# Retention in plain fp32 on parts of the array, with loads further ahead

## The chip, the cores and the metric

The kernel runs on one core of one Trainium2 chip. The metric is the device time of one execution in microseconds, median over several runs. The engines are TensorE (PE, with its weight loads shown apart as PEld), VectorE (DVE), ScalarE (ACT), GpSimd (POOL) and SyncE (SP); DMA transfers are issued from the queues of SP, ACT and POOL.

## The reference

Three layers follow one another. Inputs q, k and v have shape (8, 8, 576, 64): batch, heads, positions, head size.

```python
scores = q @ k.transpose / 8
gamma  = 1 - 2.0 ** (-5 - head)
ret    = scores * (gamma ** (i - j) where i >= j, else 0)
x      = (ret @ v), heads side by side           # 4608 rows of 512
# mixture of experts: one expert of 8 per row, by cosine similarity
e      = argmax(x/|x| @ emb/|emb|.T / tau)
y      = softmax weight of e * (relu(x @ w1[e]) @ w2[e])   # 512 -> 1024 -> 512
# dense layer
h      = y @ w_in ; out = (h * cos(h)) @ w_out             # 512 -> 2048 -> 512
```

## The kernel before

**Retention in chunks.** Each batch of 576 positions is cut into four chunks of 128 and a last one of 64 (`NCH` = 5). A chunk needs four products for its eight heads: masked scores within the chunk (k against q), a state (k times scaled v, added to the state so far), the inter-chunk part (state against q) and the intra-chunk part (scaled v against masked scores). The powers of gamma are split: v is scaled by `gk_s` on POOL ahead of the products (line 394), the output by `gq_s` on VectorE behind them (line 478), so the mask itself is one triangle.

**Units and layout.** q and k arrive with two heads on the 128 partitions (`qk`), k and v also with positions on the partitions (`kv`). `load_chunk` (line 364) issues one load of each per chunk from the SP queue; the main loop (line 641) loads `AHEAD` = 3 chunks ahead into four buffers. The scales `gq_s` are loaded one chunk's worth at a time by `load_consts` between those loads.

**Scores.** fp32 data are split in `prep_chunk` (line 378), one chunk ahead, into a high and a low fp32r part: k on ScalarE and POOL (`kx`), q on ScalarE and VectorE (`qbd`). q is laid out block-diagonally with zeros, so a matmul on the full array handles two heads, and `mm3` (line 83) multiplies high by high, high by low and low by high: 12 matmuls with 256 columns a chunk. A last chunk takes plain fp32 instead (line 429).

**State and outputs.** The state is computed for two heads at once on the full array (line 440), and its two diagonal blocks are added to the previous state in `sbd`. The inter-chunk part uses the block-diagonal state as weights (line 459), the intra-chunk part column halves of the array (line 462). The two half chunks of a pair of batches share one tile `xtail`, so 40 chunks make 36 row tiles of 128.

**Routing.** `project` (line 483) turns a row tile into row order and multiplies it by the expert embeddings, one chunk later. After a group of tiles (9, 9, 9, 5, 4) `route` and `route_rest` compute expert, rank and weight. `emit` (line 561) then, two tiles per chunk, scatters the row numbers to `idb` (POOL queue), scales the rows on ScalarE and stores them to `xd` from the SP queue. The order on POOL and ScalarE is fixed to follow the prepared chunk (`issue_after`).

**Into the experts.** After the third group, `load_rows` gathers the first 320 rows of expert 0; their transposes (`rows_to_x`, line 259) come in the last chunk, and the expert layers (lines 84 to 86) follow. Six weight pieces of expert 0 are loaded and split during the retention (`PIECE_AT`, `load_piece`, line 178). The order within each engine's queue is laid down by a planner that simulates the program; the order of the source decides where it has no reason to differ.

Of the kernel before, what the change touches and what calls it, by code (L numbers as in the profile page):

```python
# [53 lines left out]
def retention_moe_ffn(  # L54
# [72 lines left out]
    def norm_recip(T, ssq, out):  # L127
        """out = 1 / (sqrt(ssq) + 1e-6)"""
        g, r, a = T("nr_g"), T("nr_r"), T("nr_a")
        nc.vector.tensor_scalar(g, ssq, 1e-36, None, op0=ALU.max)  # L130
        nc.scalar.activation(r, g, AF.Ln)
        nc.scalar.activation(r, r, AF.Exp, scale=-0.5)
        nc.vector.tensor_tensor(a, r, r, op=ALU.mult)
        nc.vector.tensor_tensor(a, a, g, op=ALU.mult)
        nc.vector.tensor_scalar(a, a, -0.5, 1.5, op0=ALU.mult, op1=ALU.add)
        nc.vector.tensor_tensor(r, r, a, op=ALU.mult)
        nc.vector.tensor_tensor(r, r, ssq, op=ALU.mult)
        nc.vector.tensor_scalar(r, r, 1e-6, None, op0=ALU.add)
        nc.vector.reciprocal(out, r)
# [37 lines left out]

    def load_piece(src, a, pool=None):
        i = wcount[0]
        st = stage.tile([P, 1024], F32, tag="st", name=f"st{i}")  # L180
        nc.sync.dma_start(st.rearrange("p (a b) -> p a b", a=a) if a > 1 else st, src)
# [141 lines left out]
    with ExitStack() as actx:  # L323
# [14 lines left out]
        def load_consts(i):  # L338
            if i == 0:
# [4 lines left out]
                nc.gpsimd.memset(zero, 0)  # L344
            elif i <= NCH:
                nc.sync.dma_start(gq_s[:, i - 1], gq[:, i - 1])
# [3 lines left out]
        qbd = []  # L350
        for i in range(2):
            t = acon.tile([P, 2, NP, 2, CH], F32R, name=f"qbd{i}")
            for a in range(2):
                for j in range(2):
                    (nc.gpsimd if i or a else nc.vector).memset(t[(1 - j) * D : (2 - j) * D, a, :, j, :].bitcast(F32), 0.0)
            qbd.append(t)

        sbd = []
        for i in range(3):
            t = acon.tile([P, NP, P], F32, name=f"sbd{i}")  # L360
            nc.gpsimd.memset(t, 0.0)
            sbd.append(t)

        def load_chunk(b, c):
            n = CH if c < 4 else 64
            cols = slice(c * NP * CH, c * NP * CH + NP * n)
            tk = qkv.tile([P, 2, NP * CH], F32, tag="qk", name=f"qk_{b}_{c}")
            for a in range(2) if b == c == 0 else (slice(0, 2),):
                src = qk[b, a, :, cols]
                nc.sync.dma_start(tk[:, a, : NP * n], src if b == c == 0 else src.rearrange("a p n -> p a n"))  # L370
            tk = tk[:, :, : NP * n].rearrange("p a (h n) -> p a h n", h=NP)
            tv = qkv.tile([P, 2, H, D], F32, tag="kv", name=f"kv_{b}_{c}")
            nc.sync.dma_start(tv[:n].rearrange("p a h d -> p (a h d)"), kv[b, c * CH : c * CH + n, :])
            return tk, tv

        nq = [0]

        def prep_chunk(b, c, r):
            n = CH if c < 4 else 64
            tk, tv = r  # L380
            split = None
            if c < 4:
                qb = qbd[nq[0] % len(qbd)]
                nq[0] += 1
                kx = tp.tile([P, 2, NP, CH], F32R, tag="kx", name=f"kx_{b}_{c}", bufs=2)
                nc.scalar.copy(kx[:, 0], tk[:, 1])
                eng = nc.vector if b == c == 0 else nc.gpsimd
                eng.tensor_tensor(kx[:, 1], tk[:, 1], kx[:, 0], op=ALU.subtract)
                for j in range(2):
                    h = slice(j * D, (j + 1) * D)  # L390
                    state["act"] = nc.scalar.copy(qb[h, 0, :, j, :], tk[h, 0])
                    nc.vector.tensor_tensor(qb[h, 1, :, j, :], tk[h, 0], qb[h, 0, :, j, :], op=ALU.subtract)
                split = qb, kx
            state["pool"] = nc.gpsimd.tensor_tensor(
                tv[:n, 1], tv[:n, 1], gk_s[:n, c * H : (c + 1) * H].unsqueeze(2).to_broadcast([n, H, D]), op=ALU.mult
            )
            return tk, tv, split

        state = {"i": 0}
        tails = {}  # L400

        def blk(t, j):
            return t[j * D : (j + 1) * D, :, j * D : (j + 1) * D]

        def tri_f(n):
            return mask_s[:n, :n].unsqueeze(1).to_broadcast([n, 4, n])

        def chunk_scores(b, c, r):
            n = CH if c < 4 else 64
            tk, tv, split = r  # L410
            pr = []
            for a in range(2):
                sc = bank(f"sc{a}_{b}_{c}")
                t = tp.tile([P, 4, CH], F32, tag=f"p{a}", name=f"p{a}_{b}_{c}")
                if c < 4:
                    qb, kx = split
                    for p in (2 * a, 2 * a + 1):
                        mm3(
                            sc[:, (p % 2) * 256 : (p % 2 + 1) * 256],
                            lambda s: kx[:, s, p, :],  # L420
                            lambda s: qb[:, s, p].rearrange("p a n -> p (a n)"),
                            True,
                            True,
                        )
                    pr += [t[:, k, :] for k in range(4)]
                else:
                    h = slice(a * D, (a + 1) * D)
                    for p in range(NP):
                        MM(sc[:n, p * n : (p + 1) * n], tk[h, 1, p, :], tk[h, 0, p, :], start=True, stop=True)
                    pr += [t[:n, k, :n] for k in range(4)]  # L430
                nc.vector.tensor_tensor(
                    t[:n, :, :n], sc[:n, : 4 * n].rearrange("p (a n) -> p a n", a=4), tri_f(n), op=ALU.mult
                )
            prev = sbd[state["i"] % 3]
            if c < 4:
                st_ps = bank(f"st_{b}_{c}")
                k2, v2 = (tv[:, a].rearrange("p h d -> p (h d)") for a in range(2))
                for p in range(NP):
                    cols = slice(p * P, (p + 1) * P)
                    MM(st_ps[:, cols], k2[:, cols], v2[:, cols], start=True, stop=True)  # L440
                state["i"] += 1
                nxt = sbd[state["i"] % 3]
                sv = st_ps.rearrange("p (a b) -> p a b", a=NP)
                for j in range(2):
                    if c == 0:
                        nc.scalar.copy(blk(nxt, j), blk(sv, j))
                    else:
                        nc.vector.tensor_tensor(
                            blk(nxt, j), blk(sv, j), blk(prev, j), op=ALU.add
                        )  # L450
            return pr, prev

        def chunk_out(b, c, r, pr, prev):
            n = CH if c < 4 else 64
            tk, tv, split = r
            ot = bank(f"ot_{b}_{c}")
            if c > 0:
                for p in range(NP):
                    MM(ot[:, p * n : (p + 1) * n], prev[:, p, :], tk[:, 0, p, :], start=(p == 0), stop=False)
            for p in range(NP):  # L460
                for j in range(2):
                    MM(
                        ot[j * D : (j + 1) * D, p * n : (p + 1) * n],
                        tv[:n, 1, 2 * p + j, :],
                        pr[2 * p + j if c < 4 else NP * j + p],
                        start=(c == 0 and p == 0),
                        stop=(p == NP - 1),
                    )
            if c < 4:
                xt = xtp.tile([P, NP, P], F32, tag="xt", name=f"xt_{b}_{c}")  # L470
                o = 0
            else:
                g = b // 2
                if b % 2 == 0:
                    tails[g] = xtp.tile([P, NP, P], F32, tag="xtail", name=f"xtail_{g}", bufs=2)
                xt = tails[g]
                o = (b % 2) * 64
            nc.vector.tensor_tensor(
                xt[:, :, o : o + n], ot[:, : NP * n].rearrange("p (a b) -> p a b", a=NP), gq_s[:, c, :, :n], op=ALU.mult
            )  # L480
            return xt

        def project(t, xt, lp, ssq, i):
            xr = rows.tile([P, DM], F32, tag="xr", name=f"xr_{t}")
            for a in range(2):
                ps = bank(f"xn{a}_{t}")
                w = P + E
                for j in range(2):
                    p = 2 * a + j
# [493 lines left out]
```

## Time and profile before

| | us |
|---|---|
| median of 3 runs | 1576.01 (1574.17 to 1588.26) |
| profiled execution, span from its first to its last instruction | 1564.1 |
| TensorE busy in the span | 1492.1 (95%) |
| VectorE, ScalarE, POOL busy | 777.9, 629.0, 670.6 |

The page gives the span as the profiled execution's own time and no other. Retention ends at about 251 us of the span, the experts run to about 800 us and the dense layer to the end. Times in rows count from the span's start. "Idle before" names what the engine waited for. In a timeline, consecutive instructions of a kind are merged into one row; starts are measured, ends of matmuls are modelled.

### The profile page before, as it was taken

The numbers are of one execution on the slowest core, as the hardware profiler recorded it, in microseconds if no ns is written. First come the engines' busy times: TensorE is split into PE (matmuls) and PEld (weight loads), VectorE is DVE, ScalarE is ACT, GpSimd is POOL, SyncE is SP. The second block draws the span as 40 slices with busy tenths as digits, with TensorE's granted clock in tenths as the row PEclk, the third lists the DMA queues.
The fourth block names the chain that finished last, engine by engine and source line by source line (L and its number), as shares of the span: only waits on it lengthen the run. The fifth ranks groups of instructions, "written<-read, shape, count | busy, mean of one in ns | idle before, by whom it ended". The sixth has DMA issues, their size and how long they took to land.

```text
span 1564.1 us, 22887 instructions
## 1 busy us (share of the span) xinstructions
PE 1492.1 (95%) x8760; PEld 1326.3 (85%) x8760; DVE 777.9 (50%) x1357; ACT 629.0 (40%) x1120; POOL 670.6 (43%) x494
## 2 busy tenths in 40 slices
PE   8979897899999999999999999999999999999996
PEld 7968787799999899999988888888888888888885
DVE  7968685342745536556263434444444434444432
ACT  4556564242343333432363433434333334334332
POOL 5564755475565665653553223232323223232322
PEclk9998898999999999999999999999999999999998
DMA  9596974564555554544510100000000100000000
GB/s 306 180 207 208 225 185 83 148 189 151 174 169 165 168 181 162 169 153 140 192 55 7 41 7 27 27 28 27 27 28 21 34 1 27 27 28 0 28 1 27
DMA packets 118690, 157.50 MB, mean 101 GB/s; under 512 B 18984, under 2 KB 78760, under 8 KB 118576
## 3 DMA queue, kind: packets, MB, share of 16 engines
q1 hardware_dynamic: 109760, 134.58, 29.0%
q0 software_dynamic: 7360, 19.95, 3.9%
q8 instruction: 71, 1.16, 0.3%
q10 hardware_dynamic: 1456, 1.45, 0.3%
q14 instruction: 43, 0.35, 0.1%
HBM read 118.03 MB, written 38.06 MB: 100 GB/s over the span
## 4 chain that ended last, share of the span: by engine, by line
PE 51%; issue 1%; DVE 1%; ACT 0%; POOL 0%; DMA 0%; POOLq 0%; ACTq 0%; DVEq 0%
PE f L84 8%; PE f L86 8%; PE f L85 8%; PE o L84 8%; PE o L85 8%; PE o L86 8%; PE y L85 1%; PE y L86 1%; PE y L84 1%; PE h L85 0%; PE h L86 0%; PE h L84 0%; POOL g L855 0%; DMA wf<-ta 0%; DVE kk L847 0%
## 5 line engine op out<-in xcount | busy, mean ns | idle before, releaser
L855 POOL TENSOR_TENSOR g<-kk,g 128x512 fp32r<-128x512 f32 x143 | 184.5, 1291 | 509.2 <-ACT g L854 509.0
L187 POOL TENSOR_TENSOR w<-st,w 128x1024 fp32r<-128x1024 f32 x80 | 193.0, 2423 | 123.1 <-ACT w L186 119.1
L85 PE MATMUL o<-w,g 128*128 128x512 f32 x576 | 224.1, 389 | 0.0
L85 PE MATMUL f<-xf,w 128*128 128x512 f32 x576 | 224.1, 389 | 0.0
L86 PE MATMUL f<-xf,w 128*128 128x512 f32 x576 | 224.1, 389 | 0.0
L84 PE MATMUL o<-w,g 128*128 128x512 f32 x576 | 223.7, 389 | 0.2 <-DVE kk L852 0.2
L84 PE MATMUL f<-xf,w 128*128 128x512 f32 x576 | 222.5, 389 | 0.0
L850 ACT ACTIVATE sn<-kk 128x512 f32<-128x512 f32 x144 | 91.0, 632 | 320.9 <-DVE kk L848 320.5
L86 PE MATMUL o<-w,g 128*128 128x512 f32 x576 | 219.2, 389 | 0.0
L847 DVE TENSOR_SCALAR kk<-f 128x512 f32<-128x512 f32 x144 | 99.4, 691 | 230.0 <-PE f L86 221.4
L852 DVE SCALAR_TENSOR_TENSOR kk<-sn,f 128x512 f32<-128x512 f32 x144 | 98.8, 687 | 183.9 <-ACT sn L851 183.7
L85 PE MATMUL y<-hs,w 128*128 128x320 f32 x512 | 162.3, 317 | 11.6 <-DVE hs L289 11.6
L84 PE MATMUL y<-hs,w 128*128 128x320 f32 x512 | 162.7, 318 | 3.5 <-ACT hs L288 3.5
L86 PE MATMUL y<-hs,w 128*128 128x320 f32 x512 | 160.5, 314 | 0.0
L84 PE MATMUL h<-x,w 128*128 128x320 f32 x512 | 158.1, 309 | 2.4 <-PEq L725 2.4
L86 PE MATMUL h<-x,w 128*128 128x320 f32 x512 | 157.6, 308 | 0.0
L85 PE MATMUL h<-x,w 128*128 128x320 f32 x512 | 157.6, 308 | 0.0
L854 ACT CAST g<-kk 128x512 fp32r<-128x512 f32 x144 | 89.3, 621 | 113.6 <-DVE kk L852 112.8
L84 PEld LDWEIGHTS o<-w,g 128*128 128x128 f32 x576 | 108.1, 188 | 23.1 <-DVE kk L852 0.6
L86 PEld LDWEIGHTS f<-xf,w 128*128 128x128 f32 x576 | 108.2, 188 | 22.5
L85 PEld LDWEIGHTS o<-w,g 128*128 128x128 f32 x576 | 108.2, 188 | 22.4
L84 PEld LDWEIGHTS f<-xf,w 128*128 128x128 f32 x576 | 108.1, 188 | 22.4
(152 smaller groups left out, 2759.4 us busy)
## 6 DMA issues: line engine op xcount, KB each, us to landing
st<-in_moe_w_dram SPq DMA_DIRECT2D x64, 512.0 KB, 3.7
kv<-in_kv_dram SPq DMA_DIRECT2D x32, 512.0 KB, 9.1
qk<-in_qk_dram SPq DMA_DIRECT2D x31, 512.0 KB, 4.4
xs<-x2t SPq DMA_DIRECT2D x36, 256.0 KB, 2.9
x2t<-y SPq DMA_DIRECT2D x56, 160.0 KB, 3.1
xd<-xr SPq DMA_DIRECT2D x32, 256.0 KB, 9.8
sd<-in_moe_w_in_dram SPq DMA_DIRECT2D x16, 512.0 KB
wf<-ta SPq DMA_DIRECT2D x32, 256.0 KB, 2.7
```

The costliest lines, as they stand in the source:

```text
L84: keep(MM(ps, lhs(0), rhs(0), start=first, stop=False))
L85: keep(MM(ps, lhs(0), rhs(1), start=False, stop=False))
L86: keep(MM(ps, lhs(1), rhs(0), start=False, stop=last))
L187: nc.gpsimd.tensor_tensor(wt[:, 1], st, wt[:, 0], op=ALU.subtract)
L847: nc.vector.tensor_scalar(kk, ps, MAGIC, MAGIC, op0=ALU.add, op1=ALU.subtract)
L850: nc.scalar.activation(sn, kk, AF.Sin, scale=math.pi)
L852: evac = nc.vector.scalar_tensor_tensor(kk, sn, 0.5, ps, op0=ALU.subtract, op1=ALU.mult)
L854: lasti[:] = evac, nc.scalar.copy(gt[:, 0], kk)
L855: (nc.vector if (t, m) == seqf[-1] else nc.gpsimd).tensor_tensor(gt[:, 1], kk, gt[:, 0], op=ALU.subtract)
```

## The change

Scores, state and inter-chunk part become plain fp32 matmuls on parts of the array: scores on row halves (64 rows by 128 columns, one head each, halves taking turns), state on column halves (128 by 64), the inter-chunk part on quarters (64 by 64). All splits of q and k go, with the block-diagonal tiles `qbd` and `sbd`. Row and column halves exchange two heads, so `gq`, the row order in `project` and the embedding are permuted to match, and the output scale is applied in two instructions. The half chunks of two batches become one unit of 128 positions with a mask that keeps the batches apart; there are 36 units in place of 40 chunks. Loads run six units ahead with seven buffers, q and k of a unit lie together (4 KB per partition), the scales follow at distance two, `rows` has 14 buffers. The `xd` stores move from SP's queue to ScalarE's. Weight pieces are fetched at their place and split two units later. A projected tile follows one unit after its output.

```diff
+    def load_piece(src, a, pool=None):
+        return split_piece(fetch_piece(src, a, wcount[0]), pool)
...
-        rows = actx.enter_context(tc.tile_pool(name="rows", bufs=12))
+        rows = actx.enter_context(tc.tile_pool(name="rows", bufs=14))
-        qkv = qctx.enter_context(tc.tile_pool(name="qkv", bufs=4))
+        qkv = qctx.enter_context(tc.tile_pool(name="qkv", bufs=7))
...
+        def load_chunk(u):
+            tk = qkv.tile([P, 2, NP, CH], F32, tag="qk", name=f"qk_{u}")
+            for a in (slice(0, 1), slice(1, 2)) if u == 0 else (slice(0, 2),):
+                nc.sync.dma_start(tk[:, a], qk[u, :, a])
+            tv = qkv.tile([P, 2, H, D], F32, tag="kv", name=f"kv_{u}")
+            nc.sync.dma_start(tv.rearrange("p a h d -> p (a h d)"), kv[u])
...
-                nc.scalar.copy(kx[:, 0], tk[:, 1])
-                eng.tensor_tensor(kx[:, 1], tk[:, 1], kx[:, 0], op=ALU.subtract)
-                    state["act"] = nc.scalar.copy(qb[h, 0, :, j, :], tk[h, 0])
-                    nc.vector.tensor_tensor(qb[h, 1, :, j, :], tk[h, 0], qb[h, 0, :, j, :], op=ALU.subtract)
...
+        heads = [(p, a) for p in range(NP) for a in range(2)]
+        quads = [(m, a, j) for m in range(2) for a in range(2) for j in range(2)]
+        def lanes(a):
+            return slice(a * D, (a + 1) * D)
+        def chunk_scores(u, c, r):
+            sc = [bank(f"sc{a}_{u}") for a in range(2)]
+            for p, a in heads:
+                MM(sc[a][:, p * P : (p + 1) * P], tk[lanes(a), 1, p, :], tk[lanes(a), 0, p, :], start=True, stop=True)
...
+        def chunk_state(u, c, r, prev):
+            for p, a in heads:
+                MM(st_ps[lanes(a), p * D : (p + 1) * D], tv[:, 0, 2 * p + a, :], tv[:, 1, 2 * p + a, :], start=True, stop=True)
...
+                nc.vector.tensor_tensor(nxt, sv, prev, op=ALU.add)
...
+        def chunk_inter(u, c, r, prevs):
+            ot = [bank(f"ot{a}_{u}") for a in range(2)]
+            n = P // max(1, len(prevs))
+            for i, prev in enumerate(prevs):
+                for m, a, j in quads:
+                    MM(ot[a][lanes(j), m * P + i * n : m * P + (i + 1) * n],
+                       prev[lanes(a), p, :], tk[lanes(a), 0, p, i * n : (i + 1) * n], ...)
...
+        def chunk_out(u, c, r, pr, ot):
+            for m, a, j in [(m, a, j) for a in range(2) for m in range(2) for j in range(2)]:
+                MM(ot[a][lanes(j), m * P : (m + 1) * P], tv[:, 1, 2 * p + a, :], pr[a][:, p, :], ...)
+            for a in range(2):
+                nc.vector.tensor_tensor(xt[:, am, :], ot[a]..., gq_s[:, c, am, :], op=ALU.mult)
...
-                with tc.issue_after(state["pool"].ins), tc.issue_after(state["act"].ins):
+                with tc.issue_after(state["pool"].ins):
...
-                    nc.sync.dma_start(xd[row : row + P, :], xr)
+                    nc.scalar.dma_start(xd[row : row + P, :], xr)
...
-        AHEAD = 3
+        AHEAD = 6
         for i in range(AHEAD):
-            raw[seq[i]] = load_chunk(*seq[i])
-            load_consts(i)
+            raw[i] = load_chunk(i)
+            if i < 2:
+                load_consts(i)
...
+                load_consts(i + 2)
+                raw[i + AHEAD] = load_chunk(i + AHEAD)
             ...
+            pr = chunk_scores(i, c, r)
             tick(2)
...
+            ot = chunk_inter(i, c, r, [] if c == 0 else [prev] if c < NCH - 1 else [state[(b - 1, c - 1)], prev])
+            while pend:
                 rest = project_next(pend.pop(0))
...
+            if c < NCH - 1:
+                state[(b, c)] = chunk_state(i, c, r, prev)
+            xt = chunk_out(i, c, r, pr, ot)
...
+            if fetched and fetched[0][0] <= i - 2:
+                key, st = fetched.pop(0)[1:]
+                with tc.issue_after(state["pool"].ins):
+                    (w1p if key < 4 else w2p)[(0, key % 4)] = split_piece(st)
```

## Rows read from the trace of the kernel before

**Rows 1.** Windows, retention: TensorE, loads, VectorE, ScalarE, POOL busy; clock; DMA share, GB/s.

```profile
0.00:251.00 251.00, 214.09 (x1991) 194.39 (x1992) 187.95 (x425) 135.44 (x295) 135.38 (x123) 0.92 0.76 208
```

**Rows 2.** Windows, same columns: three stretches of the retention.

```profile
10.00:40.00 30.00, 27.90 (x261) 24.75 (x260) 24.20 (x48) 15.49 (x34) 14.23 (x12) 0.94 0.98 329
84.00:120.00 36.00, 23.07 (x200) 20.81 (x200) 23.43 (x34) 20.09 (x40) 24.05 (x21) 0.86 0.90 187
...
128.47:154.06 25.59, 25.21 (x259) 23.17 (x260) 23.89 (x67) 15.43 (x36) 9.95 (x9) 1.00 0.59 196
```

**Rows 3.** Timeline of TensorE, one chunk: start, length, line, shapes, count.

```profile
50.87 0.39 PE L84 MATMUL sc<-qbd,kx 128*128 128x256 f32 x1
...
51.68 1.05 PE L440 MATMUL st<-kv 128*128 128x128 f32 x8
52.57 1.09 PE L490 MATMUL xn<-rx,xt 128*128 128x136 f32 x8
53.50 1.05 PE L459 MATMUL ot<-qk,sbd 128*128 128x128 f32 x8
54.49 1.09 PE L462 MATMUL ot<-p,kv 128*64 128x128 f32 x16
55.51 0.56 PE L429 MATMUL sc<-qk 64*64 64x64 f32 x7
```

**Rows 4.** Timeline of TensorE, a half chunk, same columns.

```profile
33.72 1.00 PE L459 MATMUL ot<-qk,sbd 128*128 128x64 f32 x8
34.65 0.68 PE L462 MATMUL ot<-p,kv 64*64 64x64 f32 x16
35.26 0.51 PE L84 MATMUL sc<-qbd,kx 128*128 128x256 f32 x2
```

**Rows 5.** Timeline of all engines, 105 to 120; in brackets, idle before and releaser.

```profile
106.30 0.58 PE L86 MATMUL sc<-qbd,kx 128*128 128x256 f32 x1 [5.61 <-POOL kx L388]
...
109.42 7.31 DVE L392 TENSOR_TENSOR qbd<-qk,qbd 64x512 fp32r<-64x512 f32 x1 [9.82 <-ACT qbd L391]
...
118.91 1.34 PE L462 MATMUL ot<-p,kv 128*64 128x128 f32 x10 [6.33 <-DVE p L431]
```

**Rows 6.** Waits of the SP queue, 0 to 251: total us, times, longest.

```profile
SPq L370 <- PE ot L459: 49.5, 20, 4.8
SPq L575 <- ACT xr L570: 28.3, 16, 4.5
```

**Rows 7.** Lines by shape, 0 to 290: busy us, mean ns, idle before.

```profile
L392 DVE TENSOR_TENSOR qbd<-qk,qbd 64x512 fp32r<-64x512 f32 x64 | 67.8, 1060 | 30.0 <-ACT qbd L391 28.6
L431 DVE TENSOR_TENSOR p<-sc,misc_i 128x512 f32<-128x512 f32 x64 | 42.6, 683 | 10.3 <-PE sc L86 10.0
...
L388 POOL TENSOR_TENSOR kx<-qk,kx 128x512 fp32r<-128x512 f32 x31 | 39.7, 1282 | 50.3 <-ACT kx L386 50.1
...
L187 POOL TENSOR_TENSOR w<-st,w 128x1024 fp32r<-128x1024 f32 x12 | 29.2, 2443 | 9.3 <-ACT w L186 9.2
...
L448 DVE TENSOR_TENSOR sbd<-st,sbd 64x256 f32<-64x256 f32 x48 | 19.9, 415 | 2.0 <-PE st L440 1.4
...
L478 DVE TENSOR_TENSOR xtail<-ot,gq_s 128x256 f32<-128x256 f32 x8 | 3.4, 419 | 0.9 <-PE ot L462 0.9
```

**Rows 8.** Timeline of all engines, start: first load of scales, fourth scaled output.

```profile
3.90 0.33 SPq L346 DMA_DIRECT2D gq_s<-c_gq_dram  x1
...
32.20 0.69 DVE L478 TENSOR_TENSOR xt<-ot,gq_s 128x512 f32<-128x512 f32 x1 [0.62 <-PE ot L462]
```

**Rows 9.** Timeline of all engines, 237 to 260.

```profile
237.44 1.01 POOL L564 DMA_INDIRECT idb<-misc_i,di  x1 [0.16 <-issue]
...
243.10 0.39 SPq L244 DMA_DIRECT2D ix<-idb  x1
...
249.55 1.09 PE L266 MATMUL xt<-ident,nat 128*128 128x128 f32 x4 [6.83 <-DMA nat<-xd,ix]
...
259.59 0.40 PE L84 MATMUL h<-x,w 128*128 128x320 f32 x1
```

More of the change, by code (lines that the diff above doesn't have):

```diff
@@ L364, in load_chunk @@
[L364 to L373, printed above, removed]
+        mask_t = acon.tile([P, P], F32, name="mask_t")
@@ L394, in prep_chunk @@
             state["pool"] = nc.gpsimd.tensor_tensor(
-                tv[:n, 1], tv[:n, 1], gk_s[:n, c * H : (c + 1) * H].unsqueeze(2).to_broadcast([n, H, D]), op=ALU.mult
+                tv[:, 1], tv[:, 1], gk_s[:, c * H : (c + 1) * H].unsqueeze(2).to_broadcast([P, H, D]), op=ALU.mult
             )
[L397 to L406, printed above, removed]
@@ L411, in chunk_scores @@
             pr = []
             for a in range(2):
[L413 to L430, printed above, removed]
+                t = tp.tile([P, NP, CH], F32, tag=f"p{a}", name=f"p{a}_{u}")
@@ new lines, in chunk_scores @@
+                nc.vector.tensor_tensor(t, sc[a].rearrange("p (a n) -> p a n", a=NP), tri, op=ALU.mult)
+                pr.append(t)
+            return pr
+        def chunk_state(u, c, r, prev):
+            tk, tv = r
+            st_ps = bank(f"st_{u}")
+            for p, a in heads:
+                MM(
+                    st_ps[lanes(a), p * D : (p + 1) * D],
+                    tv[:, 0, 2 * p + a, :],
+                    tv[:, 1, 2 * p + a, :],
+                    start=True,
+                    stop=True,
+                )
+            nxt = tp.tile([P, NP, D], F32, tag="s", name=f"s_{u}", bufs=4)
+            sv = st_ps[:, : NP * D].rearrange("p (a b) -> p a b", a=NP)
+            if c == 0:
+                nc.scalar.copy(nxt, sv)
+            else:
+                nc.vector.tensor_tensor(nxt, sv, prev, op=ALU.add)
+            return nxt
@@ new lines, in chunk_inter @@
+        def chunk_inter(u, c, r, prevs):
+            tk, tv = r
+            ot = [bank(f"ot{a}_{u}") for a in range(2)]
+            n = P // max(1, len(prevs))
+            for i, prev in enumerate(prevs):
+                for m, a, j in quads:
+                    p = 2 * m + j
+                    MM(
+                        ot[a][lanes(j), m * P + i * n : m * P + (i + 1) * n],
+                        prev[lanes(a), p, :],
+                        tk[lanes(a), 0, p, i * n : (i + 1) * n],
+                        start=(m == 0 and i == 0),
+                        stop=False,
+                        skip_group_check=True,
+                    )
+            return ot
@@ new lines, in chunk_out @@
+        def chunk_out(u, c, r, pr, ot):
+            tk, tv = r
+            for m, a, j in [(m, a, j) for a in range(2) for m in range(2) for j in range(2)]:
+                p = 2 * m + j
+                MM(
+                    ot[a][lanes(j), m * P : (m + 1) * P],
+                    tv[:, 1, 2 * p + a, :],
+                    pr[a][:, p, :],
+                    start=(c == 0 and m == 0),
+                    stop=(m == 1),
+                    skip_group_check=True,
+                )
+            xt = xtp.tile([P, NP, P], F32, tag="xt", name=f"xt_{u}")
+            for a in range(2):
+                am = slice(2 * a, 2 * a + 2)
@@ L431, in chunk_scores @@
                 nc.vector.tensor_tensor(
-                    t[:n, :, :n], sc[:n, : 4 * n].rearrange("p (a n) -> p a n", a=4), tri_f(n), op=ALU.mult
+                    xt[:, am, :], ot[a][:, : 2 * P].rearrange("p (m q) -> p m q", m=2), gq_s[:, c, am, :], op=ALU.mult
                 )
[L434 to L480, printed above, removed]
@@ L487, in project @@
                 w = P + E
-                for j in range(2):
-                    p = 2 * a + j
-                    MM(ps[:, j * w : (j + 1) * w], xt[:, p, :], rx[:, p, :], start=True, stop=True)
+                for m in range(2):
+                    MM(ps[:, m * w : (m + 1) * w], xt[:, 2 * a + m, :], rx[:, 2 * a + m, :], start=True, stop=True)
                 pv = ps[:, : 2 * w].rearrange("p (a b) -> p a b", a=2)
@@ L600, in prepare_experts @@
                 nc.vector.tensor_copy(rx[:, c, :P], ident)
-        seq = [(b, c) for b in range(B) for c in range(NCH)]
+        seq = [(b, c) for b in range(B) for c in range(NCH) if c < NCH - 1 or b % 2]
         raw = {}
@@ L921, in _layout, with units @@
 def _layout(q, k, v):
-    t = [a.reshape(B, NP, P // D, S, D).transpose(0, 2, 4, 1, 3).reshape(B, P, NP, S) for a in (q, k)]
-    t = np.stack(t, axis=2)
-    t = t.transpose(0, 2, 1, 3, 4)
-    qk = np.concatenate([t[..., c * CH : (c + 1) * CH].reshape(B, 2, P, -1) for c in range(NCH)], axis=3)
-    kv = np.stack([a.transpose(0, 2, 1, 3) for a in (k, v)], axis=2).reshape(B, S, 2 * DM)
-    return dict(qk=qk, kv=kv)
+    def units(a, axis):
+        cut = [slice(c * CH, (c + 1) * CH) for c in range(NCH)]
+        at = lambda b, c: a[b][(slice(None),) * axis + (cut[c],)]
+        for b in range(B):
+            yield from (at(b, c) for c in range(NCH - 1))
+            if b % 2:
+                yield np.concatenate([at(b - 1, NCH - 1), at(b, NCH - 1)], axis=axis)
+    t = [a.reshape(B, NP, P // D, S, D).transpose(0, 2, 4, 1, 3).reshape(B, P, NP, S) for a in (q, k)]
+    qk = np.stack([np.stack(list(units(a, 2))) for a in t], axis=2)
+    kv = np.stack([np.stack(list(units(a.transpose(0, 2, 1, 3).reshape(B, S, DM), 0))) for a in (k, v)], axis=2)
+    return dict(qk=qk, kv=kv.reshape(NTILE, P, 2 * DM))
 def _consts():
```

84 lines of the change are left out of this document (35 added, 49 removed).

## The prediction

> **What bounds the kernel now.** I read the windows first. The retention stage, 0 to 251 us, keeps TensorE busy for 214.09 of 251 us at a mean granted clock of 0.92, with the DMA engines at a share of 0.76 [rows 1]. All that the change touches lies ahead of the first uninterrupted expert matmul at 259.59 [rows 9]; the 1304.5 us behind it I take over unchanged.
>
> Inside the stage there are two regimes. A batch without a disturbance, 128.47 to 154.06, has TensorE busy for 25.21 of 25.59 us at clock 1.00 [rows 2]: TensorE sets the pace, 25.6 us for four chunks and a half one. The timeline shows how a full chunk fills it, by differences of starts: scores in fp32r 0.81 us for six matmuls (1.62 for twelve), state 0.89, projection 0.93, inter-chunk part 0.99, intra-chunk part 1.02, together 5.4 us [rows 3]. The second regime is 84 to 120: TensorE busy 23.07 of 36 us, clock 0.86, DMA share 0.90 but only 187 GB/s, where 10 to 40 has 329 GB/s at share 0.98 [rows 2]. There the scores waited 5.61 us for POOL's split of k, and the next output 6.33 us for masked scores; these stood on VectorE behind one split of q that took 7.31 us [rows 5], where the mean is 1.06 [rows 7]. Eight batches at 25.6 are 205 us, so some 45 of the first 251 us are start-up, such stalls and the slow clock behind them.
>
> The SP queue shows why data come late: its q and k loads waited 49.5 us in all for old buffers to be read out, and the xd stores, in the same queue with the loads behind them, 28.3 us for ScalarE's scaling [rows 6].
>
> **The change, part by part.**
>
> *The splits of q and k go.* VectorE loses two instructions a chunk, 67.8 us in all; POOL loses 39.7 us [rows 7]; ScalarE its casts. VectorE keeps per unit two masks at 0.683, a state sum in one instruction (0.42) and the output scale in two halves (0.42 each, as the 256-column row) [rows 7]: 2.6 us and the routing's small ones, below any TensorE pace here. What is late next is TensorE itself, or the raw load.
>
> *TensorE.* In the trace an fp32 matmul is two instructions; eight of them on the full array take 0.89 us, 0.111 each [rows 3]. Column halves run side by side: sixteen take 1.02 us [rows 3], which is 16 x 0.056 and 0.13 more at the change of array shape. Quarters with 64 columns, two at once: sixteen in 0.61 us [rows 4], 0.038 each, or 16 x 0.028 and 0.17. I charge 0.15 for a change of shape. Per new unit:
> - State, sixteen on column halves with 64 columns: 0.61, as that row.
> - Output, column halves as before: 1.02. Projection as before: 0.93.
> - Inter-chunk, sixteen on quarters with 128 columns: between 0.028 (four at once) and 0.056 (two at once) each; I take the middle, 0.042, so 0.67 + 0.15 = 0.82.
> - Scores, sixteen on row halves with 128 weight columns: no row has row halves taking turns. Side by side they would cost 0.056 each, one by one 0.111. For the upper end speaks that the full-array inter-chunk part with 64 moving columns takes 0.93 us for eight [rows 4], hardly less than 0.99 with 128 [rows 3]: something other than the moving columns binds there. For the lower end speaks that quarters overlap. I take 0.076, twice the 0.038 of the 64-column quarter, the nearest row: 1.22 + 0.15 = 1.37.
>
> Sum 4.75 us, against 5.4 for a full chunk, and nine units replace ten chunks of two batches. A batch's first unit has no inter-chunk part (0.8 less, seven of the 30 units counted below), a joined unit no state, but 32 short inter matmuls (0.4 less, three): 6.8 us off in all. A unit changes the array's shape once or twice more than a chunk did, and the 0.15 is charged each time. The Trainium skill, TensorEngine Tiling (Array Packing), section Key Properties, says that a change of tiling mode drains the engine, which speaks against this change; it gives no price, and with a drain as long as the 0.15 us read from the rows the sum stays as it is.
>
> *Six units ahead, seven buffers, xd stores on ScalarE's queue.* The load of unit i+6 needs the buffer of unit i-1, long read out, and no store stands ahead of it. A store now stands on ScalarE behind its own scaling and delays what follows there; at 0.33 us an issue, as the 256 KB load shown [rows 8], two a unit in a burst are 0.7 us, covered by a ScalarE that is busy 15.43 of 25.59 us even with the casts [rows 2]. If that cover fails, the copies of the projection come 0.7 us later in some 14 burst units: 10 us at most. POOL's scatters no longer wait for ScalarE, only for the POOL scaling of the next unit's v, whose load is now early. Splitting a weight piece two units after its fetch moves POOL and ScalarE work off a landing; cost nothing, POOL being busy for 9.95 of 25.59 us [rows 2]; uncovered, 2.4 us for each of six pieces [rows 7].
>
> *Start-up, late next.* The output scales gq of chunks 1 to 3 used to be issued between the first loads; now the first of them stands behind six units, 6 x 1.05 MB, and 0.4 MB of constants, at 329 GB/s [rows 2] some 21 us after the first microsecond, and each next one behind one more unit (1.31 MB, 4 us). So the scaled outputs of units 1, 2 and 3 can't come before 22, 26 and 30 us, though no split stands ahead of the first scores any more. Before, the fourth came at 32.20 [rows 8]. I take 30.
>
> *DMA in the three bursts.* By the last load 51 MB have moved (37.7 q, k and v, 7.1 xd, 4.7 weight pieces, 1.5 constants). Nine units with a burst of stores are 12.6 MB: 38 us at 329 GB/s, under TensorE's 42. If 7.6 MB of them move at 187 GB/s it is 41 + 15 us, 14 late a cycle, 42 in three, of which the lead of six units (28 us) hides all but 14. I take 4, and keep 0 and 14.
>
> *End.* The chain keeps its length: last scatter of the third group at 237.44, its indices read from 243.10, first transposes at 249.55, dense expert matmuls at 259.59: 22 us [rows 9]. As before, one unit lies between scatter and transposes, so TensorE still waits there.
>
> **Sum.** 30 (fourth output) + 30 units x 4.75 - 6.8 + 1.4 (scores of the 35th unit) = 167; + 22 = 189; + 4 (bursts); + 3 for small waits (TensorE's 25.59 - 25.21 us a batch [rows 2], eight times) = 196 us for the first dense expert matmul, 64 us earlier than 259.59. The profiled span is 1564.1 us; the median of the runs is 11.9 more, which I take for what lies around the span. 1564.1 - 64 + 11.9 = **1512 us**.
>
> **Rivals.**
> - *Row halves don't overlap.* Scores at 0.111 and inter at 0.056 each: 0.8 us a unit more, 24 us: 1536. For it, the 64-column row above. The Trainium skill, TensorE: Matmul & The Clock Gate, section LDWEIGHTS, has a rule that would cause it: a weight load's time goes by its columns, not its rows, and the scores still load 128 columns; at its figure, an estimate of 107 ns a load, the time is about the same. The trace agrees on the full array alone. Chance 0.20.
> - *DMA late by its upper end.* The bursts cost 14 and the start-up 5 more: 1527. For it, the 187 GB/s; against it, the lead. Chance 0.16.
> - *Slower.* With a queue of their own the xd stores mix with the loads at all times, and the 187 GB/s of a burst becomes the stage's rate: 51 MB take 273 us, and with 18 us of the end chain behind the last load the experts start at 291, 31 us later than now: 1607. It decides from 211 GB/s down (51 MB in 241.6 us). Against it, the stage averages 208 GB/s with the DMA engines free for a quarter of the time [rows 1]. Chance 0.08.
> - *It doesn't do what it says.* Loads wait elsewhere (behind constants, for buffers), and the time saved on TensorE turns into waiting for data; only a part of the stalls goes, up to 11 of the 45 us: 1565 to 1576. Chance 0.08.
>
> **How the numbers follow.** The forecast has 0.48. Within 1% (1560 to 1592, about what a measurement can't tell from no change) lies the last case, slower the third: faster 0.84, same 0.08, slower 0.08. The low end takes 0.056 and 0.028 for the two open prices (16 us less), no late burst (4) and an earlier start (4): 1488. The high end takes serial row halves and late bursts together: 1546, and 4 more for ScalarE in the bursts: 1550.
>
> **What would show it.** Scores: sixteen row-half matmuls in 1.0 to 1.4 us if right, 1.8 or more if they don't overlap. Pace: outputs of neighbouring units 4.2 to 5 us apart in undisturbed stretches. TensorE waits over 5 us for data only in the first 30 us and once at the end. First dense expert matmul near 196, the same 1304 us behind it. I am wrong if windows between 60 and 160 us show TensorE well under 0.9 busy with a DMA share near 1, if the granted clock there lies for long at its lower level of 1.2 GHz, or if the expert stage grows.

## The result, and the profile after

| | before | after |
|---|---|---|
| median on the same chip, us | 1579.98 (1574.17 to 1588.26) | 1535.07 (1532.43 to 1535.38) |
| span of the profiled execution, us | 1564.1 | 1533.5 |
| first expert matmul of the profiled execution, us | 258.05 | 220.00 |

The ratio is 0.9714, 95% interval 0.9676 to 0.9753: faster by some 45 us, where 64 were forecast. 1535 lies inside the range, 23 above the predicted 1512. The experiments show that one thing costs more than the whole miss: the way the row numbers (ids) are scattered into their table. I had seen it in the trace of before and put it down to another cause. The 258.05 and 220.00 are the first expert matmuls of all, with the projection of the last tile still behind them. The prediction counts from 259.59, behind that projection and 1.5 us later, so its 196 answers to 194.5 here.

**Where the forecast holds.** The timeline of TensorE, one unit of after in a quiet stretch (start, length, line, shapes, count); it answers to [rows 3, 4]:

```profile
41.02 1.16 PE L386 MATMUL sc<-qk 64*128 64x128 f32 x16
42.12 0.67 PE L421 MATMUL ot<-qk,s 64*64 64x128 f32 x16
42.71 1.19 PE L458 MATMUL xn<-rx,xt 128*128 128x136 f32 x8
43.84 0.69 PE L399 MATMUL st<-kv 128*64 128x64 f32 x16
44.35 1.05 PE L435 MATMUL ot<-p,kv 128*64 128x128 f32 x16
```

By differences of starts: scores 1.10, inter-chunk part 0.59, projection 1.13, state 0.51, and 0.98 up to the next scores at 45.33: 4.31 us a unit. The fourth scaled output, which answers to the last of [rows 8], comes at 29.83 (VectorE's timeline; the first stands in the same view):

```profile
12.40 0.74 DVE L446 TENSOR_TENSOR xt<-ot,gq_s 128x256 f32<-128x256 f32 x2
...
29.83 0.86 DVE L446 TENSOR_TENSOR xt<-ot,gq_s 128x256 f32<-128x256 f32 x2
40.70 0.86 DVE L446 TENSOR_TENSOR xt<-ot,gq_s 128x256 f32<-128x256 f32 x2
```

**Where it does not.** Windows of after (the columns of [rows 1]): the retention stage, a quiet stretch, and the stretch with the first two groups of scatters.

```profile
0.00:251.00 251.00, 208.10 (x2707) 177.15 (x2708) 129.81 (x418) 96.41 (x232) 97.14 (x93) 0.89 0.74 223
...
145.00:175.00 30.00, 29.70 (x492) 25.44 (x490) 22.33 (x68) 10.60 (x30) 14.24 (x10) 0.98 0.86 311
...
66.00:145.00 79.00, 60.01 (x780) 49.13 (x776) 35.61 (x109) 30.73 (x74) 34.83 (x31) 0.85 0.92 219
```

VectorE and POOL have lost 58 and 38 us against [rows 1], about as forecast, though this window of after has some 30 us of the expert stage in it. But from 66 to 145 TensorE is busy for 60 of 79 us with the DMA engines at a share of 0.92 and only 219 GB/s. From the fourth output to the 34th (29.83 to 206.72) 30 units take 5.9 us each. In that stretch POOL issues nine scatters in a row, and TensorE does the scores of one unit in pieces (timelines of POOL and of TensorE; in brackets the idle time before and its end):

```profile
67.95 1.14 POOL L532 DMA_INDIRECT idb<-misc_i,di  x1 [0.32 <-DVE lp L463]
...
78.23 0.96 POOL L532 DMA_INDIRECT idb<-misc_i,di  x1 [0.31 <-issue]
```

```profile
72.58 0.64 PE L386 MATMUL sc<-qk 64*128 64x128 f32 x2
73.68 0.47 PE L386 MATMUL sc<-qk 64*128 64x128 f32 x3 [0.46 <-issue]
74.38 0.27 PE L386 MATMUL sc<-qk 64*128 64x128 f32 x1 [0.23 <-issue]
...
80.22 0.80 PE L386 MATMUL sc<-qk 64*128 64x128 f32 x3 [1.04 <-issue]
```

Sixteen matmuls that take 1.10 us elsewhere are spread from 72.58 to 81.0. "issue" says that nothing which the profile shows was waited for; the waits of TensorE, 0 to 224 us (total, times, longest), have 20.5 us of it, of which the three largest are

```profile
PE xn L458 <- issue: 6.5, 5, 2.2
PE sc L386 <- issue: 6.4, 12, 1.0
PE st L399 <- issue: 6.1, 6, 2.0
```

The end, answering to [rows 9] (all engines; the last scatter of the third group, the reading of its indices, the transposes, the first expert matmul):

```profile
188.99 0.96 POOL L532 DMA_INDIRECT idb<-misc_i,di  x1 [0.30 <-issue]
196.38 0.38 SPq L250 DMA_DIRECT2D ix<-idb  x1
...
211.25 1.48 PE L272 MATMUL xt<-ident,nat 128*128 128x128 f32 x12
...
220.00 0.64 PE L84 MATMUL h<-x,w 128*128 128x320 f32 x1
```

### The profile page after: what moved, and what is told of

It is laid out like the page before. It is cut to its first block, busy times and chain, and to the rows that moved or that the text cites. A ratio compares the mean times of both kernels' runs of the same rounds, so it can differ in the third digit from the quotient of the medians.

```text
span 1533.5 us, 23567 instructions
## 1 busy us (share of the span) xinstructions
PE 1456.4 (95%) x9272; PEld 1281.2 (84%) x9272; DVE 696.9 (45%) x1294; ACT 569.6 (37%) x1016; POOL 616.5 (40%) x450
## 3 DMA queue, kind: packets, MB, share of 16 engines
q8 instruction: 75, 1.23, 0.3%
## 4 chain that ended last, share of the span: by engine, by line
PE 53%; DVE 1%; issue 1%; DMA 1%; POOL 1%; ACT 1%; POOLq 0%; ACTq 0%; DVEq 0%
PE f L85 8%; PE f L84 8%; PE f L86 8%; PE o L84 8%; PE o L85 8%; PE o L86 8%; PE y L85 1%; PE y L86 1%; PE y L84 1%; DMA wf<-ta 1%; PE h L85 1%; PE h L86 1%; PE h L84 1%; POOL w L193 0%; POOL g L837 0%
## 5 line engine op out<-in xcount | busy, mean ns | idle before, releaser
L193 POOL TENSOR_TENSOR w<-st,w 128x1024 fp32r<-128x1024 f32 x74 | 177.9, 2415 | 120.3 <-ACT w L192 120.1
L84 PE MATMUL h<-x,w 128*128 128x320 f32 x512 | 160.1, 313 | 4.3 <-DVEq L707 4.3
L85 PE MATMUL h<-x,w 128*128 128x320 f32 x512 | 159.4, 311 | 0.0
L86 PE MATMUL h<-x,w 128*128 128x320 f32 x512 | 159.4, 311 | 0.0
```

Of the source, the lines that this page charges most:

```text
L84: keep(MM(ps, lhs(0), rhs(0), start=first, stop=False))
L85: keep(MM(ps, lhs(0), rhs(1), start=False, stop=False))
L86: keep(MM(ps, lhs(1), rhs(0), start=False, stop=last))
L193: nc.gpsimd.tensor_tensor(wt[:, 1], st, wt[:, 0], op=ALU.subtract)
```

## The experiments

Twelve kernels ran, in three sets, each set beside the kernel before on one chip; ratios are to that, and the changed kernel's own is 0.9714 (0.9676 to 0.9753). In the cuts of code, "..." stands for lines left out. One window, 66 to 145 us, compares them: in the changed kernel 780 matmuls, 219 GB/s.

My first theory (A) was that nine scatters in a row starve the other engines, since the change had removed the wait that spread them. Four kernels undo one part each.

**e1_paced**: scatters and row scalings again wait for ScalarE's last copy.

```diff
-                nc.scalar.copy(xv[:, a], ...)
+                state["act"] = nc.scalar.copy(xv[:, a], ...)
...
+                    tc.add_manual_dep(ins.ins, state["act"].ins.name, ..., reason="pace")
+                    with tc.issue_after(state["act"].ins):
-                    nc.scalar.mul(xr, xr, gt[:, i : i + 1])
+                        nc.scalar.mul(xr, xr, gt[:, i : i + 1])
```

> The changed kernel, with the pacing of the emits put back: each scatter on GpSimd and each scaling of a row on ScalarE is issued only behind the copy of the last projected tile on ScalarE, as in the kernel before; stores, lead and matmuls stay as in the changed kernel. Theory A (the nine scatters run back to back, from 67.95 to 79.2, 126.1 to 137.2 and 178.9 to 190 us, and beside them every engine is slow to get its instructions, at a loss of 10 to 13 us in a burst): the scatters come in small groups again, the three stretches shrink, and the first dense expert matmul comes at 185 to 200 us in place of 223.7; about 1505 us, ratio to before 0.955. Rival B (the loads and the stores on two queues share the DMA engines; scatters are innocent): the stretches stay, 1530 to 1540 us, ratio 0.97. Rival C (pacing keeps ScalarE or GpSimd waiting for the projection and holds up the next value scaling): slower than the changed kernel, 1540 to 1560 us.

Measured: 1542.86 us, ratio 0.9739 (0.9706 to 0.9771). The scatters of the first group did spread (two at 67 to 69 us, six from 80 to 88, one at 106), and the time did not fall. Windows, first 66 to 145, then a stretch with the last scatter of the first group:

```profile
66.00:145.00 79.00, 58.62 (x872) 49.59 (x866) 39.62 (x116) 31.81 (x78) 34.22 (x29) 0.87 0.95 219
...
92.00:112.00 20.00, 5.65 (x92) 4.73 (x92) 4.53 (x10) 0.94 (x1) 4.52 (x4) 0.75 1.07 160
```

TensorE waits less for "issue" (6.2 us in place of 20.5, 0 to 224) and 26.5 us (30 to 224) for ScalarE, whose queue waits for late weight pieces (timeline of ScalarE):

```profile
84.52 1.04 ACT L192 CAST w<-ste 128x1024 fp32r<-128x1024 f32 x1 [8.27 <-DMA ste<-in_moe_w_dram]
...
111.06 1.04 ACT L192 CAST w<-ste 128x1024 fp32r<-128x1024 f32 x1 [20.09 <-DMA ste<-in_moe_w_dram]
```

So A falls: spacing changes who is late; from 66 to 145 the DMA engines moved the same 219 GB/s.

**e2_paced_scatter**: only the scatters wait.

```diff
...
+                    tc.add_manual_dep(ins.ins, state["act"].ins.name, ..., reason="pace")
```

> Only the scatters on GpSimd wait for the copy of the last projected tile on ScalarE; the row scalings and their stores run free as in the changed kernel. Theory A: most of the gain of the run with both paced, 1505 to 1515 us (ratio 0.955 to 0.96). Rival B, and the rival that it is the bunched row scalings and stores of ScalarE and not the scatters: no gain, 1530 to 1540 us.

Measured: 1552.29 us, ratio 0.98 (0.9766 to 0.9835): slower than the changed kernel. A is wrong here too.

**e2b_paced_store**: only the scalings, and with them the stores, wait.

```diff
...
-                    nc.scalar.mul(xr, xr, gt[:, i : i + 1])
+                    with tc.issue_after(state["act"].ins):
+                        nc.scalar.mul(xr, xr, gt[:, i : i + 1])
```

> Only the row scalings of ScalarE, and with them the stores, stay behind the copy of the last projected tile; the scatters run back to back as in the changed kernel. Theory A: 1525 to 1540 us, the stretches with scatters stay as long. Rival (bunched stores are the cause): 1505 to 1515 us with the scatters as bunched as before.

Measured: 1534.61 us, ratio 0.9685 (0.965 to 0.9719). Bunched stores are not the cause.

**e3_xd_on_sp**: the row stores back on SP's queue.

```diff
-                    nc.scalar.dma_start(xd[row : row + P, :], xr)
+                    nc.sync.dma_start(xd[row : row + P, :], xr)
...
```

> The changed kernel with the row stores back on SP's queue behind the loads; nothing else. Theory A: the scatters are as bunched, 1530 to 1545 us. Rival B (stores on a queue of their own mix with the loads and slow them): the loads keep their rate, the scores' stalls go, 1505 to 1515 us. A third reading, that the stores on SP are waited for by the loads behind them: 1545 to 1565 us.

Measured: 1538.55 us, ratio 0.9695 (0.9661 to 0.973), and 211 GB/s from 66 to 145. It matters neither way which queue the stores are on; rival B falls.

What was left in all four were the scatters themselves. The second set doubles them, puts them off, and changes what they write (theory D).

**e8_double**: a second scatter behind each, into a table that nothing reads.

```diff
+                    ins2 = nc.gpsimd.indirect_dma_start(
+                        out=idb2[:, :],
+                        out_offset=bass.IndirectOffsetOnAxis(ap=di[:, i : i + 1], axis=0),
+                        in_=ids_s[:, t0 + i : t0 + i + 1], in_offset=None)
...
```

> The changed kernel with every scatter of ids followed by a second one of the same kind into a table that nothing reads: 36 more scatters, 27 of them in the retention. Theory D (the scatters slow the DMA engines for all others: from 72 to 90 us they moved 90 to 170 GB/s at a busy share of 0.8 to 1.0, where loads alone moved 390; with them the loads and TensorE's instructions come late, whatever the scatters' spacing): the three stretches lose as much again, 10 to 15 us each; the first expert matmul at 250 to 265 us, 1562 to 1580 us, ratio 0.99 to 1.00. Rival E (the scatters are innocent and the stretches come from the turn of weights, stores and queues): only GpSimd's time counts, of which there is enough: 1533 to 1545 us.

Measured: 1558.67 us, ratio 0.9884 (0.9855 to 0.9912), some 27 us more than the changed kernel by the ratios; a little under the range, far above the rival's. The long window:

```profile
66.00:145.00 79.00, 54.45 (x775) 46.18 (x772) 35.54 (x107) 29.59 (x73) 41.02 (x38) 0.83 0.95 208
```

**e6_defer**: the first two groups' scatters put off to the third's.

```diff
...
+                late.append(lambda: scatter(i))
+                if g >= EARLY:
+                    while late:
+                        late.pop(0)()
...
```

> The changed kernel with the scatters of ids of the first two groups put off until those of the third, so that 27 run in a row near the end of the retention, and none before; row scalings and stores stay. Theory D: without scatters the units go at 4.3 to 4.6 us through what were the first two stretches, unit 24 or so is out some 20 to 25 us earlier; the 18 late scatters cost 18 x 1.26 = 23 us on GpSimd ahead of the ids of the first expert, plus the slow DMA: 1530 to 1550 us in all, with the gain visible in the units alone. Rival E: the stretches around 70 and 130 us stay as they are although no scatter runs there, and the whole is 1555 to 1575 us.

Measured: 1539.8 us, ratio 0.9761 (0.9727 to 0.9795). Windows: without scatters, and beside the late run of 27, which POOL issues from 151.45 to 197.27:

```profile
66.00:145.00 79.00, 69.28 (x1052) 59.15 (x1050) 45.73 (x132) 35.60 (x87) 27.91 (x20) 0.91 0.78 267
...
160.00:170.00 10.00, 6.62 (x98) 5.42 (x94) 5.03 (x14) 3.98 (x8) 4.06 (x5) 1.00 0.83 107
170.00:180.00 10.00, 0.00 (x0) 0.00 (x0) 0.00 (x0) 0.94 (x3) 4.42 (x5) 0.58 1.07 122
```

The slow DMA stretch went where the scatters went. The 24th output came at 134.44 in place of 149.22 us, 15 us earlier and not the 20 to 25 I expected: from 66 to 145 TensorE still waited 7.8 us for ScalarE's copies, so not every stop there comes from scatters. TensorE stood still from 170 to 180, and the whole gained nothing.

**e7_wide**: each id written as 16 equal words, in rows of 64 bytes.

```diff
+W = 16
-    idb = dram.tile([E * NT, 1], I32, name="idb")
+    idb = dram.tile([E * NT, W], I32, name="idb")
...
-                        in_=ids_s[:, t0 + i : t0 + i + 1],
+                        in_=idw[:, t0 + i, :],
...
```

> The changed kernel with each id written as 16 equal words, in a table with rows of 64 bytes: as many scatters, as many descriptors, the same time of GpSimd, but 64 bytes for each in place of 4. The table is 16 times as large, its zeros are written later, and a row buffer fewer is there (13 of 14). If what slows the DMA engines is that words of 4 bytes, many of them neighbours, are written into memory: the slow stretches nearly go, 1495 to 1515 us. If it is the number of descriptors, or GpSimd's writing of them: 1530 to 1550 us with the same stretches.

Measured: 1500.32 us, ratio 0.9518 (0.95 to 0.9537): 31 us below the changed kernel by the ratios, 34.7 by the spans. POOL still issues nine scatters in a row at the same pace (74.72 to 85.08). Windows of e7_wide, the long stretch and the two with scatters, then its first expert matmul (timeline of TensorE):

```profile
66.00:145.00 79.00, 70.78 (x1112) 60.24 (x1108) 52.34 (x152) 37.42 (x92) 44.59 (x39) 0.96 0.86 289
...
74.00:90.00 16.00, 15.01 (x240) 12.81 (x236) 10.88 (x28) 8.01 (x21) 13.22 (x13) 1.00 0.91 333
122.00:138.00 16.00, 14.78 (x238) 12.62 (x235) 10.41 (x27) 8.78 (x23) 13.23 (x14) 1.00 0.92 331
```

```profile
194.32 0.41 PE L85 MATMUL h<-x,w 128*128 128x320 f32 x1
```

TensorE is busy for 15 of 16 us beside the scatters, and its "issue" waits fall from 20.5 to 3.0 us. The scatters are as many and as bunched, so GpSimd's work and the number of descriptors do not cost the time; what is written, or where, does. The edit also gives the second table of ids (`idl`, copied from the first in the expert stage) the wide rows; with this, the later zeros and the missing row buffer, it is not a change of one thing, but e6_defer and e8_double tie the slow stretches to the scatters without any of that.

**e5_scales_first**: the output scales ahead of units 2 to 5.

```diff
+            if i == 1:
+                for k in (2, 3, 4):
+                    load_consts(k)
...
-                load_consts(i + 2)
+                if i + 2 > 4:
+                    load_consts(i + 2)
```

> The changed kernel with the output scales of chunks one to three loaded right behind the second unit, ahead of units 2 to 5; nothing else. My reading of the start (outputs at 12.4, 23.4, 26.3, 29.8 us, each with its scales behind six units): units 1 to 3 come out by 16 to 24 us, TensorE is 5 to 8 us ahead at 30 us, and if the slow stretches only lose what they lose now, 1527 to 1532 us. Rival (the retention is bound by the DMA engines from the start, so what TensorE gains at the start it waits for later): 1533 to 1538 us.

Measured: 1529.72 us, ratio 0.9697 (0.9652 to 0.9742), not to be told from the changed kernel. The start went as read (the fourth output at 24.93 in place of 29.83):

```profile
24.93 0.86 DVE L446 TENSOR_TENSOR xt<-ot,gq_s 128x256 f32<-128x256 f32 x2
```

The 4.9 us gained there are gone by the first expert matmul, which came at 220.52 (220.00 in the changed kernel), as the rival had it; by the times alone the two readings are not told apart.

The last set asks whether the kernel before paid too, what of a 4-byte write hurts, and what the lead is worth.

**b1_before_wide**: the kernel before with ids of 64 bytes (the edit of e7_wide, without its loss of a row buffer).

```diff
-    idb = dram.tile([E * NT, 1], I32, name="idb")
+    idb = dram.tile([E * NT, W], I32, name="idb")
...
-                        in_=ids_s[:, t0 + i : t0 + i + 1],
+                        in_=idw[:, i, :],
...
```

> The kernel before, with each id written as 16 equal words (64 bytes) as in e7_wide. It tells whether the slow DMA stretches were already in the time before. If they were hidden there (the kernel before took 6.2 us for a unit and left the DMA engines a third of their time): 1565 to 1580 us, ratio 0.99 to 1.00, and what the change took off TensorE met them only afterwards. If the kernel before paid for them as the changed one does: 1535 to 1550 us, ratio 0.975 to 0.98, and the change alone is then worth what e7_wide is below this run.

Measured: 1554.52 us, ratio 0.987 (0.982 to 0.992), between my two cases. The kernel before paid some 20 us by the ratio (13 to 28 by its interval); the spans give 13 (1564.1 to 1551.3), but 1564.1 is less than any span recorded for before beside the experiments (1569.3 and up). The stretch with its first scatters, 90 to 130 us, before and then b1_before_wide:

```profile
90.00:130.00 40.00, 27.90 (x223) 25.44 (x222) 27.14 (x37) 18.59 (x38) 23.79 (x18) 0.79 0.89 198
```

```profile
90.00:130.00 40.00, 32.63 (x291) 29.55 (x290) 34.08 (x52) 26.85 (x55) 32.03 (x26) 0.87 0.76 252
```

**e10_pitch**: the table of e7_wide, but each scatter writes one word of 4 bytes to the head of its 64-byte row. The cut is against e7_wide.

```diff
-                        out=idb[:, :],
+                        out=idb.rearrange("n (o w) -> (n o) w", w=1),
...
-                        in_=idw[:, t0 + i, :],
+                        in_=ids_s[:, t0 + i : t0 + i + 1],
...
-            nc.vector.tensor_copy(di, df)
+            nc.vector.tensor_scalar(di, df, float(W), None, op0=ALU.mult)
...
```

> As e7_wide, with the same table of 64-byte rows, but each scatter writes only the first word of its row: 4 bytes again, no two of them in the same 64 bytes. If what hurts is many words of one 64-byte stretch written one after the other: as fast as e7_wide, 1497 to 1507 us. If any write of 4 bytes hurts, wherever it goes: 1530 to 1545 us.

Measured: 1503.42 us, ratio 0.9549 (0.9497 to 0.96), as e7_wide. The long window and the first nine scatters:

```profile
66.00:145.00 79.00, 72.76 (x1145) 62.10 (x1144) 51.79 (x154) 37.45 (x92) 44.99 (x39) 0.94 0.86 289
...
74.00:90.00 16.00, 15.06 (x246) 12.87 (x246) 9.74 (x24) 6.93 (x19) 13.09 (x12) 1.00 0.91 329
```

Words of 4 bytes are as cheap as 64 bytes when each has 64 bytes to itself. In the packed table the 128 rows of a scatter fall into up to eight runs of consecutive places, one for each expert, so on average some 16 of its words are neighbours. The scatters themselves show it too: the median from issue to landing, 0 to 260 us, is 11.8 us in the kernel before and 3.0 in b1_before_wide, and 4.4 and 3.9 in e7_wide and e10_pitch. The spaced table is also 16 times as large, so that it is the neighbouring words, and not the smaller stretch of memory written, is not shown by itself.

**e4_lead3**: three units ahead, four buffers, ids packed.

```diff
-        qkv = qctx.enter_context(tc.tile_pool(name="qkv", bufs=7))
+        qkv = qctx.enter_context(tc.tile_pool(name="qkv", bufs=4))
...
-        AHEAD = 6
+        AHEAD = 3
```

> The changed kernel with loads three units ahead and four buffers in place of six and seven, ids in words of 4 bytes. If the lead of six carries TensorE over the slow DMA stretches (theory D): they bite deeper, 1540 to 1560 us. If the lead is worth nothing, or only makes the start-up longer because the scales stand behind six units: 1525 to 1536 us.

Measured: 1556.38 us, ratio 0.9882 (0.9822 to 0.9942). So the longer lead, with its buffers, is worth some 26 us here by the ratios, 21 by the medians. Waits of TensorE, 30 to 224 us:

```profile
PE xn L458 <- ACT xr L464: 34.4, 5, 11.2
```

**e9_combined**: e7_wide, the scales early, the zeros of the table later, weight pieces split four units behind their load. This cut too is against e7_wide.

```diff
...
-            if i == 8:
+            if i == 11:
...
+            if i == 1:
+                for k in (2, 3, 4):
+                    load_consts(k)
...
-            if fetched and fetched[0][0] <= i - 2:
+            if fetched and fetched[0][0] <= i - 4:
...
```

> e7_wide with three more steps: the output scales of chunks one to three ahead of units 2 to 5, the zeros of the table three units later (in e7_wide the outputs stop from 35.5 to 47.5 us beside them), and the first expert's weight pieces split four units behind their load in place of two. Start 5 us earlier, 5 us less beside the zeros, 5 us less where ScalarE waited for weights: 1484 to 1495 us. If the retention is bound by the DMA engines once the ids are wide: as e7_wide, 1495 to 1503 us.

Measured: 1499.06 us, ratio 0.9512 (0.9466 to 0.9558), not to be told from e7_wide. Its first expert matmul came at 189.94 in place of 194.32, and from 30 to 66 the DMA engines were full with loads, 377 GB/s:

```profile
30.00:66.00 36.00, 35.47 (x584) 30.08 (x581) 27.59 (x80) 17.52 (x43) 9.40 (x9) 1.00 1.06 377
```

## Why the prediction was right in sign and 23 us off

- **Splits**: right. VectorE and POOL are no longer near any bound [rows 1 against the first window of after].
- **TensorE, 4.75 us a unit**: measured 4.31. Scores 1.10 (taken 1.37), inter-chunk part 0.59 (0.82), state 0.51 (0.61), output 0.98 (1.02), projection 1.13 (0.93). I had priced the two unknown terms too high and the projection too low. **Row halves do overlap**, 0.069 us a matmul, where the rival had 0.111, so it is out. The rule that I had cited for it, from the Trainium skill, TensorE: Matmul & The Clock Gate, section LDWEIGHTS, gives an estimate of 107 ns for a load of 128 columns, or 1.7 us for sixteen one after another; these scores load 128 columns each and take 1.10.
- **Six units ahead at no cost**: right, and worth 21 to 26 us beside packed ids (e4_lead3). The pacing that POOL's scatters lost costs nothing: putting it back saved no time (e1_paced, e2_paced_scatter). Weight pieces at no cost: not right; ScalarE waited for them 18.4 us in after and 19.4 in e7_wide, and TensorE behind it 3.7 (at 104.24) and 5.5 (at 96.14 and 99.99). What that costs in the end was not tried by itself; e9_combined splits them later, among other things, and is no faster.
- **Start-up at 30 us**: 29.83; e5_scales_first shows the cause as named.
- **DMA in the three bursts, 4 us (0 to 14)**: this step failed. By e7_wide the packed ids cost 31 us by the ratios, 34.7 by the spans: 25.7 of the 34.7 ahead of the first expert matmul (220.00 against 194.32), where the term stood, and 9.0 behind it. I read the 187 GB/s at share 0.90 [rows 2] as the rate of loads mixed with stores and charged it to the stores' bytes. The runs show that it is the rate beside packed 4-byte ids, bunched or spread, and that the stores' queue and bunching do not matter. The upper bound of 14 was worked from the wrong cause, and from 7.6 MB for which no row stands, and so was too low.
- **The stalls of before** [rows 2, 5], which I put down to splits and queue order, were in part the same thing: the kernel before loses some 20 us to it (b1_before_wide).
- **End chain, 22 us**: the first expert matmul stands 20.6 us behind the last scatter of the third group in before, 31 in after, 19 in e7_wide (175.37 to 194.32). In after the reading of the ids starts 7.4 us behind that scatter, in e7_wide 3.6 (at 179.00), and the last three outputs came only at 206.72, 209.96 and 219.26, so TensorE's late units and not the chain alone set that time.
- **The same 1304 us behind it**: from the first expert matmul on it was 1306.0 in before and 1313.5 in after, so the expert stage and what follows grew by 7.5, another of my signs of being wrong; in e7_wide 1304.5.
- **11.9 us around the span**: wrong. In the runs of after it is about 1.9 (1535.38 less 1533.5), and so it is in those of before; the profiled execution of before was simply a short one, as the 21 spans recorded for before beside the experiments start at 1569.3.

Put together: 1512 + 25.5 (220.00 for 194.5) + 7.5 - 10.0 (1.9 for 11.9) = 1535. The last term hid a third of what I had missed, which was luck. Without it the forecast is 1502, near what the kernel takes once the ids are not packed (1500, first expert matmul at 194.32); that is in part luck too, as the terms differ: units 0.44 us faster, thirty times, against stops that I had not counted. The packed ids bring it to 1535. Between kernels with wide ids the change is worth 0.9518 / 0.987, or 3.6%.

Of the rivals, "row halves don't overlap" (1536) met the time by chance, as the measured price refutes it; "DMA late" (1527) was nearest in mechanism and wrong in source; "slower" fell with the result, and e3_xd_on_sp shows that the stores' queue is not what the loads suffer from. My own sign of being wrong, TensorE well under 0.9 busy between 60 and 160 us with a DMA share near 1, came up.

Open: what TensorE's "issue" waits are (0 to 224 us). In the changed kernel and its variants they come to 1.3 to 3.0 us with ids at a pitch of 64 bytes and to 4.2 to 23.6 with packed ones; the kernel before, with packed ids, has none. Where they are small with packed ids (e1_paced, e4_lead3, e6_defer), TensorE waits for ScalarE's copies instead, 20 to 34 us from 30 to 224. Its instructions come through the DMA engines too (the page lists a queue of the kind instruction with 75 packets and 1.23 MB), so late instructions are a likely reading, but none of the runs isolates it. Nor was another pitch than 64 bytes tried.

## What to carry to other kernels

A DMA share near 1 at half the usual GB/s is a symptom, not a load: ask which transfer in that stretch writes the smallest pieces side by side, and change where it writes before changing when. A table that is filled by small scatters can pay for its compactness; give each entry 64 bytes of its own, and read only the first word of each, as these kernels do. Where a trace shows a bad rate, find out by an edit what makes it before pricing a change by it: removing compute around it did not remove the rate here.

## What the hardware showed

Scattered 4-byte writes into a packed table hold up the transfers beside them: 219 GB/s over 79 us with 18 such scatters, 289 with the same scatters at a pitch of 64 bytes, whether 4 or 64 bytes were written. The Trainium skill, DMA: Bandwidth & Descriptors, section Specifications, has transfers under 512 bytes below line rate, because the DMA engine then reads, modifies and writes. By that alone packed, spaced and 64-byte ids would cost alike; here 64 bytes, and 4 bytes at that pitch, let the DMA engines move 329 to 333 GB/s in the stretches with scatters, so the measurement decides.

Eight fp32 matmuls, each two instructions in the trace, take 1.10 us on row halves (64 by 128) with 128 moving columns, and 0.59 on quarters with 128 moving columns, hardly more than the state's eight on column halves with 64 (0.51).
